# A decode kernel that streams its K and V cache: the MLP's weights first, sums in four column groups, and other sizes for wo and the last V

## The chip, the core and the metric

The kernel runs on one NeuronCore of a Trainium2 chip. The metric is the time of one execution in device microseconds: 1358.99 us, the median of three runs (1357.01 to 1359.01). A NeuronCore has a matrix engine (TensorE, PE in the profile, with PEld for its weight loads), VectorE (DVE), ScalarE (ACT), GpSimd (POOL) and SyncE (SP), which here does nothing but issue transfers. Sixteen DMA engines move data between HBM and the on-chip memory SBUF. Each engine works through its own instructions in order and waits for others by semaphores; an SP that waits for one transfer's buffer issues none of the transfers behind it. The matrix engine's sums go to PSUM.

## The reference

Two rows of activations x (2 x 1024, bf16) go through two branches, and a gate mixes them.

```python
def _A_ref(x, k_cache, v_cache, wq, wo):
    B, Sq, D = x.shape                       # 2, 1, 1024
    H, Dh = 32, 128
    q = (lambda x, *d: x.transpose(*d))((x @ wq).reshape(B, Sq, H, Dh), 0, 2, 1, 3)
    scores = jnp.einsum("bhqd,bhkd->bhqk", q, k_cache) * (Dh ** -0.5)
    p = _softmax(scores, axis=-1)            # over 16384 keys
    o = jnp.einsum("bhqk,bhkd->bhqd", p, v_cache)
    return (lambda x, *d: x.transpose(*d))(o, 0, 2, 1, 3).reshape(B, Sq, H * Dh) @ wo
...
    h = _gelu(_layernorm(x, axis=-1) @ w1)   # then h's four quarters are shifted along S
    hs = jnp.concatenate([g0, g1, g2, g3], axis=-1) @ w2
    x1 = x + hs
    h2 = _gelu(_layernorm(x1, axis=-1) @ w3) @ w4
    return x1 + h2
...
    g = _sigmoid((x * gate_w).sum(-1, keepdims=True))
    return g * a + (1 - g) * b
```

K and V are 2 x 32 x 16384 x 128 in bf16, 268 MB each. wq and wo are 1024 x 4096 and 4096 x 1024, w1 and w2 1024 x 1024, w3 and w4 1024 x 3584 and 3584 x 1024. The sequence has one position, so every shifted quarter of h is zero, and so is hs: the kernels multiply a zero row (shT) by w2 all the same.

## The kernel before

**Units.** The cache is worked through in 32 units: a pair of heads of one batch row, 16 pairs x 2 rows. A unit's K is 8.39 MB and lies in SBUF as 128 partitions of 64 KB; its V likewise. One large SBUF tile `mem` is cut into five cells of 32 KB per partition. K of even units takes cells 0 and 1, K of odd units cells 1 and 2, V cells 3 and 4.

**What a unit does.** `score_first` and `score_second` go through K in 8 chunks: VectorE turns a chunk in 32 x 32 blocks (L464, 2.28 us), TensorE multiplies it by q (L470, 8 matmuls of 512 columns). The half that lies in cell 1 goes first, since the next unit's K needs that cell. `softmax_a` finds the maxima; `pv` multiplies an earlier unit's probabilities by its V (64 matmuls, L542); `pv_end` scales the sums on ScalarE (osb) and brings them to a column per head by 4 matmuls with lane selectors (L560); `softmax_b` makes the exponentials. pv of unit n - 2 runs in unit n, after which the next V may be loaded. After each second unit `wo_project` (L432) adds the pair's two heads times wo into `arow`, two PSUM rows of 512 columns each.

**The MLP** lies inside units 0 and 1. w1 and w2 take cell 2, w3 takes the cells of wq after the q projection, w4 those of w3. A layer accumulates in `oacc`, four rows r at a time in four groups of 32 partitions (L210, `wide_bank`), is copied to `wide`, and is summed over the groups and turned by one fp32 matmul with a 128 x 128 left side for each 128 outputs (L241; L275 for q). `layernorm_T`, `gelu_T` and the gate are short chains of small instructions. The fourth layer and the residual reach `arow` by L409.

**The order of transfers** is the order in which SP meets them: wq, x, gate_w, K of unit 0, w1, w2; w3 after the q projection; K1, wo of four heads, w4, K2, V0, K3, V1 and so on: K and V alternate. wo comes four heads at a time, 2 KB to a row. From unit 29 six small reads of gate_w ("probe", L447) are issued among the others; all write the same tile, so each waits for the one before to land. The last V is cut in eleven pieces (32, 32, 32, 32, 32, 32, 16, 16, 16, 8, 8 of 256 columns j) that go to cells 3 and 4, and the last wo pair comes behind them. `pv_last` multiplies the first 96 columns as `pv` does and the other 160 with V as the left side (L587). Two copies (L643, L645) and two output transfers end the program.

Of the kernel before, what the change touches and what calls it, by code (L numbers as in the profile page):

```python
# [10 lines left out]
FP32 = mybir.dt.float32  # L11
# [12 lines left out]
def kernel(  # L24
# [26 lines left out]

# [4 lines left out]
    CT = 32  # L56
# [6 lines left out]
    assert NJ % CT == 0 and CT % GT == 0 and NG <= QP  # L63
# [3 lines left out]
    wopool = ctx.enter_context(tc.tile_pool(name="wopool", bufs=1))  # L67
# [3 lines left out]
    sps = ctx.enter_context(tc.tile_pool(name="sps", bufs=2, space=PSUM))  # L71
    ops = ctx.enter_context(tc.tile_pool(name="ops", bufs=1, space=PSUM))
    rps = ctx.enter_context(tc.tile_pool(name="rps", bufs=1, space=PSUM))
# [8 lines left out]
    def region(cell, elements):  # L82
        return mem[:, cell * CELL : cell * CELL + elements]

    k_cell = [0 if u % 2 == 0 else 1 for u in range(NU)]
    v_cell = [3] * NU
    v_cell[NU - 2] = 0
    units = [(hp, b) for hp in range(HP) for b in range(B)]

    def cache_rows(cache, u):  # L90
        hp, b = units[u]
        return cache[b, 2 * hp : 2 * hp + 2].rearrange("h s d -> (h s) d").rearrange(
            "(p j) d -> p (j d)", p=P
        )

    def load_k(u):
        nc.sync.dma_start(out=region(k_cell[u], NJ * Dh), in_=cache_rows(A_k_cache, u))

    def load_v(u):
        nc.sync.dma_start(out=region(v_cell[u], NJ * Dh), in_=cache_rows(A_v_cache, u))  # L100

    PIECES = [32] * 6 + [16] * 3 + [8] * 2
    assert sum(PIECES) == NJ

    def load_v_pieces(u):
        j = 0
        for n in PIECES:
            nc.sync.dma_start(
                out=region(v_cell[u], NJ * Dh)[:, j * Dh : (j + n) * Dh],
                in_=cache_rows(A_v_cache, u)[:, j * Dh : (j + n) * Dh],  # L110
            )
            j += n

    def k_view(u):
        return region(k_cell[u], NJ * Dh).rearrange("p (j d) -> p j d", d=Dh)

    def v_view(u):
        return region(v_cell[u], NJ * Dh).rearrange("p (j d) -> p j d", d=Dh)

    wq_t = region(3, KC * H * Dh).rearrange("p (r n) -> p r n", r=KC)  # L120
    nc.sync.dma_start(out=region(3, KC * H * Dh), in_=A_wq.rearrange("(p r) n -> p (r n)", p=P))
    xin = const.tile([P, B, KC], BF16)
    nc.sync.dma_start(out=xin[:], in_=A_x.rearrange("b s (p r) -> p (b s) r", p=P))
    gwT = const.tile([P, KC], BF16)
    nc.sync.dma_start(out=gwT[:], in_=gate_w.rearrange("(p r) -> p r", p=P))
    load_k(0)
# [12 lines left out]
    sel = const.tile([P, 4, Q4, QP], BF16)  # L139
    nc.gpsimd.memset(sel[:], 0.0)  # L140
    for v in range(4):
        w, e = divmod(v, 2)
        nc.gpsimd.affine_select(
            out=sel[:, v],
            in_=sel[:, v],
            compare_op=ALU.not_equal,
            fill=1.0,
            base=-(2 * QP * w + e),
            pattern=[[0, Q4], [-2, QP]],
            channel_multiplier=1,  # L150
        )
# [9 lines left out]
    )  # L161

# [11 lines left out]
    sel8 = const.tile([P, 8], FP32)  # L174
    nc.vector.tensor_reduce(
        out=sel8[:],
        in_=ident_f[:].rearrange("p (c k) -> p k c", k=QP)[:, 0:8, :],
        axis=AX.X,
        op=ALU.add,
    )  # L180
    oacc = [ops.tile([P, 4 * Dh], FP32, name=f"oacc{k}") for k in range(2)]
    for k in range(2):
        nc.vector.memset(oacc[k][:], 0.0)

    NW = 2
    WW = P + NG
    qw = []
    for k in range(NW):
        t = const.tile([P, 4, WW], BF16, name=f"qw{k}")
        nc.gpsimd.memset(t[:], 0.0)  # L190
        qw.append(t)
# [485 lines left out]
```

## Time and profile before

| | |
|---|---|
| runs, median (range) | 1358.99 us (1357.01 to 1359.01) |
| profiled execution, span | 1358.0 us |
| mean granted clock of TensorE | 0.785 |
| PE busy | 806.9 us, 59% |
| VectorE busy | 650.4 us, 48% |
| ScalarE busy | 133.5 us, 10% |
| GpSimd busy | 15.2 us, 1% |
| read from HBM | 572.53 MB, 422 GB/s over the span |
| queue q1 (SP's transfers), share of the 16 DMA engines | 98.1% |
| K transfers, issue to landing (median) | 28.2 us |
| V transfers, issue to landing (median) | 33.5 us |

The page cuts the span in 40 slices of 34 us and gives for each the busy tenths of an engine and the rate of the transfers. A window's row says the same for a chosen stretch: its length, the busy time of each engine with its number of instructions, the granted clock of TensorE (1.00 is full speed), the mean busy share of the DMA engines, and GB/s. A transfer is counted where its packets start, so a share of a short window can pass 1. In a timeline a row is the start, the duration, the engine, the line, the operation, and in brackets how long the engine had been idle and what ended that. A row of waits gives who waited for whom, the total, how often and the longest. Issue to landing holds the wait behind earlier transfers.

### The profile page before, as it was taken

The page shows a single profiled execution, that of the slowest core. Times are in us where ns is not written, and L with a number is a line of the kernel's source. Part 1 is how long each engine was busy: PE and PEld are TensorE (multiplying, and loading weights), DVE is VectorE, ACT ScalarE, POOL GpSimd, SP SyncE. Part 2 cuts the span into 40 slices and gives each one's busy share as a digit, 9 for nine tenths or more (in the row PEclk, how much of TensorE's full clock was granted, in tenths as well). Part 3 has the DMA queues.
Part 4 walks back from the last instruction along what each step waited for, and adds up shares of the span by engine and source line. Part 5 has one row for each costly group of instructions (what it writes and reads, how often), then busy time and mean ns, then how long its engine had stood idle before and what let it go on. Part 6 is the DMA issues. An engine that isn't in the chain of part 4 may idle for free.

```text
span 1358.0 us, 11505 instructions
## 1 busy us (share of the span) xinstructions
PE 806.9 (59%) x5086; PEld 366.8 (27%) x5086; DVE 650.4 (48%) x511; ACT 133.5 (10%) x208; POOL 15.2 (1%) x54
## 2 busy tenths in 40 slices
PE   2897855555665545566555556655456665555564
PEld 1463422222222222222222222222222222222222
DVE  1436654444555534455544445555344555444450
ACT  0011011111100111110011111001111100111110
POOL 1000000000000000000000000000000000000000
PEclk9977877778876768888777788877678886777886
DMA  9987999999999999999999999999999999999996
GB/s 402 433 360 315 431 433 433 431 431 427 433 433 432 424 438 433 435 435 426 436 433 433 431 429 433 431 431 428 433 431 429 433 427 432 435 435 435 425 424 277
DMA packets 16183, 573.26 MB, mean 422 GB/s; under 512 B 1922, under 2 KB 1926, under 8 KB 6662
## 3 DMA queue, kind: packets, MB, share of 16 engines
q1 hardware_dynamic: 16130, 572.54, 98.1%
q8 instruction: 39, 0.64, 0.2%
q14 instruction: 10, 0.08, 0.0%
q10 hardware_dynamic: 4, 0.00, 0.0%
HBM read 572.53 MB, written 0.00 MB: 422 GB/s over the span
## 4 chain that ended last, share of the span: by engine, by line
DMA 67%; PE 17%; DVE 12%; issue 3%; ACT 0%; SPq 0%; POOL 0%; DVEq 0%; ACTq 0%
DMA mem<-in_A_k_cache_dram 57%; PE S L470 12%; DVE KT L464 11%; DMA probe<-in_gate_w_dram 7%; PE misc L241 2%; DMA xin<-in_A_x_dram 2%; PE oacc L210 1%; PE misc L275 1%; DMA wo<-in_A_wo_dram 1%; DMA mem<-in_A_v_cache_dram 0%; PE oacc L542 0%; PE arow L409 0%; ACT pt L509 0%; ACT mem L201 0%; DVE wide L203 0%
## 5 line engine op out<-in xcount | busy, mean ns | idle before, releaser
L470 PE MATMUL S<-KT,qw 128*128 128x512 bf16 x2048 | 551.9, 420 | 385.0 <-DVE KT L464 384.6
L464 DVE STREAM_TRANSPOSE KT<-mem 128x2048 f32<-128x2048 f32 x256 | 571.4, 2283 | 297.3 <-DMA mem<-in_A_k_cache_dram 243.6
L470 PEld LDWEIGHTS <-qw 128*128 128x128 bf16 x2048 | 219.8, 108 | 711.0 <-issue 537.0
L542 PE MATMUL oacc<-mem,pt 128*8 128x512 bf16 x2008 | 115.5, 382 | 8.6 <-DMA mem<-in_A_v_cache_dram 8.6
L495 ACT ACTIVATE Dm<-ident_s,m 128x128 f32<-128x128 f32 x32 | 12.8, 401 | 983.6 <-DVE m L493 983.6
L509 ACT ACTIVATE pt<-St,nb 64x256 bf16<-64x256 f32 x64 | 89.7, 1402 | 73.3 <-DVE nb L507 65.7
L572 DVE TENSOR_SCALAR OT<-misc,g_rep 128x2 bf16<-128x2 f32 x31 | 6.9, 222 | 140.5 <-PE misc L560 140.5
L520 PE MATMUL misc<-rs,lmat 128*128 128x1 f32 x62 | 17.8, 356 | 87.0 <-ACT pt L509 87.0
L542 PEld LDWEIGHTS <-pt 128*8 128x8 bf16 x2008 | 46.2, 87 | 74.5 <-issue 23.6
L522 DVE RECIPROCAL rinv<-misc 128x1 f32<-128x1 f32 x31 | 5.2, 168 | 101.6 <-PE misc L520 101.6
L491 DVE STREAM_TRANSPOSE St<-S 128x512 f32<-128x512 f32 x32 | 22.9, 717 | 63.7 <-PE S L470 63.7
L560 PE MATMUL misc<-sel,osb 128*128 128x2 f32 x256 | 34.5, 257 | 26.7 <-ACT osb L555 26.7
L560 PEld LDWEIGHTS misc<-sel,osb 128*128 128x128 f32 x256 | 31.8, 195 | 42.9 <-ACT osb L555 42.9
L520 PEld LDWEIGHTS misc<-rs,lmat 128*128 128x128 f32 x62 | 15.1, 303 | 97.9 <-ACT pt L509 97.7
L509 ACT ACTIVATION_READ_ACCUMULATOR pt<-St,nb 64x1 f32 x64 | 30.6, 478 | 0.0
L555 ACT ACTIVATE osb<-oacc,rinv 128x512 f32<-128x512 f32 x31 | 21.3, 687 | 69.0 <-PE oacc L542 69.0
L210 PE MATMUL oacc<-mem,xT 128*2 128x512 bf16 x64 | 9.4, 612 | 24.0 <-DVE xT L266 23.2
L307 POOL TENSOR_TENSOR qw<-qd,mask 128x16 bf16<-128x16 bf16 x32 | 8.4, 266 | 1180.9 <-PE S L470 1137.3
L507 DVE TENSOR_REDUCE nb<-misc 64x1 f32<-64x64 f32 x64 | 14.2, 222 | 5.0 <-PE misc L501 0.9
L275 PEld LDWEIGHTS misc<-sel,wide 128*128 128x128 f32 x64 | 14.2, 328 | 7.4 <-issue 4.4
L203 DVE COPY wide<-oacc 128x512 f32<-128x512 f32 x7 | 4.8, 691 | 22.9 <-PE oacc L210 22.9
L501 PE MATMUL misc<-Dm,ones_f 128*128 128x128 f32 x64 | 15.6, 326 | 0.0
(96 smaller groups left out, 168.3 us busy)
## 6 DMA issues: line engine op xcount, KB each, us to landing
mem<-in_B_w_dram SPq DMA_DIRECT2D x2, 7168.0 KB, 25.0
wo<-in_A_wo_dram SPq DMA_DIRECT2D x7, 1024.0 KB, 32.8
mem<-in_A_v_cache_dram SPq DMA_DIRECT2D x6, 1024.0 KB, 5.9
mem<-in_B_w_dram SPq DMA_DIRECT2D x2, 2048.0 KB, 45.9
mem<-in_A_v_cache_dram SPq DMA_DIRECT2D x3, 512.0 KB, 14.3
wo<-in_A_wo_dram SPq DMA_DIRECT2D x2, 512.0 KB
mem<-in_A_k_cache_dram SPq DMA_DIRECT2D x32, 28.2
mem<-in_A_v_cache_dram SPq DMA_DIRECT2D x2, 256.0 KB, 14.0
```

The source lines that it names most:

```text
L210: nc.tensor.matmul(acc[QP * q : QP * q + B, :], lhsT=actT[:, r, :], rhs=weight[:, r, :], start=(r < Q4), stop=(r >= R - Q4),)
L241: nc.tensor.matmul(ps[:, c, :], lhsT=wide.rearrange("p (m c) -> p c m", c=self.C)[:, c, :], rhs=sel8[:, 0:B], start=True, stop=True,)
L275: nc.tensor.matmul(qps[:, j * HB + k, :], lhsT=qo[:, k * Dh : (k + 1) * Dh], rhs=sel8[:, 0:B], start=True, stop=True,)
L464: nc.vector.transpose(out=kt[:], in_=Kc.rearrange("p j d -> p (j d)").bitcast(FP32))
L470: nc.tensor.matmul(S, lhsT=t[:, v, NG - 1 - m : NG - 1 - m + P], rhs=ktb[:, half * GT : (half + 1) * GT, w, :, e], start=(first and n == 0 ...
L491: nc.vector.transpose(out=st[:].rearrange("p j r -> p (j r)"), in_=S[:])
L501: nc.tensor.matmul(R_ps[:], lhsT=ones_f[:], rhs=Dm[:], start=True, stop=True)
L509: nc.scalar.activation(out=Pt[rows, :, e, :].rearrange("p (m a) k -> p a k m", a=GT // 4), in_=st[rows, :, 0:NG].rearrange("p (a k) m -> p ...
L520: nc.tensor.matmul(tot_ps[:, 0:1], lhsT=lmat[:], rhs=rs[:], start=True, stop=True)
L542: nc.tensor.matmul(acc[QP * q : QP * q + 8, :], lhsT=pts[u % NP][:, g].rearrange("p h k -> p (h k)"), rhs=v_view(u)[:, 4 * g : 4 * g + 4, ...
L555: nc.scalar.activation(out=osb[:], in_=oacc[u % 2][:], func=ACTF.Copy, scale=rinvs[u % NP][:, 0:1] if scaled else 1.0,)
L560: nc.tensor.matmul(ot[:], lhsT=osb[:, k * Dh : (k + 1) * Dh], rhs=sel8[:, k : k + 5 : 4], start=(k == 0), stop=(last and k == 3),)
```

## The change

- **Start.** x and gate_w are issued by ScalarE's queue. SP issues w1, w2 (cell 0), w3 (cells 1 and 2) and wq (cells 3 and 4) first, all without a wait; then K of unit 0 (cells 0 and 1, when w1 to w3 have been used), w4 (when wq has been used), K of unit 1, V of unit 0, the first wo pair. The gate, both layer norms and the first three layers come before the q projection and before any score; the fourth layer (`mlp_last`) stands in unit 0 behind its scores, and the residual times 1 - g (x1g) is added to `arow` ahead of the third layer.
- **Sums in column groups.** `rows4` gives each of the four 32-partition groups a quarter of the output's columns, so that every group holds finished sums. They are turned by one VectorE transpose (`turned`) instead of 128 x 128 matmuls. `arow` becomes one PSUM tile of 256 columns in four groups, written by 8 matmuls of 256 columns for a pair (`project`) and by 112 for the fourth layer (28 rows x 4 groups).
- **Units.** pv of unit n - 1 runs in unit n. V of unit n is issued behind it. The halves of a unit are put into `odd_rest` and `even_unit`; K and V still alternate in the queue.
- **wo** comes a pair at a time as 128 rows of 4 KB (two neighbouring rows of wo in a partition) into one buffer, `wo_pair`, issued after the previous pair's `project`. So that the columns fit, `pv_end` splits even and odd lanes: 16 small fp32 matmuls with 64 columns of left side, for 4 with 128. Pair 15 is fetched this way too, but is used from a second transfer in the old layout (`wo_last`).
- **End.** The last V goes to cells 0 and 1 in five pieces of 128, 64, 32, 16 and 16 columns; 192 columns go as in `pv`, 64 with V as the left side. wo's last pair goes to cell 3. One copy and two output transfers of four rows of 512 bytes end the program. The probes are gone.

```diff
-    k_cell = [0 if u % 2 == 0 else 1 for u in range(NU)]
-    v_cell = [3] * NU
-    v_cell[NU - 2] = 0
-    units = [(hp, b) for hp in range(HP) for b in range(B)]
...
-    PIECES = [32] * 6 + [16] * 3 + [8] * 2
...
+    xin = const.tile([P, B, KC], BF16)
+    nc.scalar.dma_start(out=xin[:], in_=A_x.rearrange("b s (p r) -> p (b s) r", p=P))
+    gwT = const.tile([P, KC], BF16)
+    nc.scalar.dma_start(out=gwT[:], in_=gate_w.rearrange("(p r) -> p r", p=P))
+
+    def load_weight(W, cell, offset=0):
+        K, N = W.shape
+        dst = region(cell, K // P * N, offset)
+        nc.sync.dma_start(out=dst, in_=W.rearrange("(p r) n -> p (r n)", p=P))
+        return dst.rearrange("p (r n) -> p r n", n=N)
+
+    w1 = load_weight(B_w1, 0)
+    w2 = load_weight(B_w2, 0, KC * D)
+    w3 = load_weight(B_w3, 1)
+    wq = load_weight(A_wq, 3)
+
+    K_CELL = (0, 1)
+    V_CELL = 3
...
-    nc.sync.dma_start(out=region(3, KC * H * Dh), in_=A_wq.rearrange("(p r) n -> p (r n)", p=P))
-    xin = const.tile([P, B, KC], BF16)
-    nc.sync.dma_start(out=xin[:], in_=A_x.rearrange("b s (p r) -> p (b s) r", p=P))
-    gwT = const.tile([P, KC], BF16)
-    nc.sync.dma_start(out=gwT[:], in_=gate_w.rearrange("(p r) -> p r", p=P))
-    load_k(0)
...
+    def rows4(acc, actT, weight, R, at, n, G):
         for r in range(R):
...
+            for g in range(Q4):
                 nc.tensor.matmul(
+                    acc[QP * g : QP * g + B, 0:n],
+                    lhsT=actT[:, r, :],
+                    rhs=weight[:, r, g * G + at : g * G + at + n],
+                    start=(r == 0),
+                    stop=(r == R - 1),
                 )
...
+    def turned(wide, C):
+        t = mlp.tile([P, C, QP], FP32, tag="turn", name="turn")
+        nc.vector.transpose(
+            out=t[:].rearrange("p c k -> p (c k)"), in_=wide.rearrange("p c k -> p (c k)")
+        )
+        return t[:, :, 0:B]
+
+    def layer(actT, weight, k):
+        rows4(oacc[k], actT, weight, KC, 0, G1, G1)
+        wide = mlp.tile([P, KC, QP], FP32, tag="wide", name="wide")
+        nc.scalar.activation(
+            out=wide[:], in_=oacc[k][:, 0:G1].rearrange("p (i r) -> p r i", r=KC), func=ACTF.Copy
+        )
+        return turned(wide[:], KC)
...
+    compute_gate()
+    layernorm_T(xT[:], xn1T[:], "ln1")
+    h1 = gelu_T(layer(xn1T, w1, 0), KC)
+    nc.vector.tensor_copy(out=hT[:], in_=h1[:])
+
+    nc.vector.memset(shT[:], 0.0)
...
+    nc.vector.tensor_tensor(out=x1T[:], in0=layer(shT, w2, 1), in1=xT[:], op=ALU.add)
+    layernorm_T(x1T[:], xn2T[:], "ln2")
+
+    for k in range(2):
+        rows4(oacc[k], xn2T, w3, KC, k * (G3 // 2), G3 // 2, G3)
+    wide3 = mlp.tile([P, FC, QP], FP32, tag="wide", name="wide")
+    for k in range(2):
...
+    wo_pair = const.tile([P, 2, D], BF16, name="wo_pair")
+
+    def load_wo(hp):
+        rows = A_wo[bass.ds(hp * 2 * Dh, 2 * Dh)]
+        nc.sync.dma_start(
+            out=wo_pair[:].rearrange("p t n -> p (t n)"),
+            in_=rows.rearrange("(p t) n -> p (t n)", p=P),
+        )
...
+    def project(oT, weight, last):
+        for t in range(2):
+            for g in range(Q4):
                 nc.tensor.matmul(
+                    arow[QP * g : QP * g + B, :],
+                    lhsT=oT[:, t, :],
+                    rhs=weight[:, t, g * G1 : (g + 1) * G1],
+                    start=False,
+                    stop=(last and t == 1),
+                    skip_group_check=True,
+                )
...
+    def mlp_last(w4):
+        for r in range(KC):
+            for g in range(Q4):
+                nc.tensor.matmul(
+                    arow[QP * g : QP * g + B, :].rearrange("b (i r) -> b r i", r=KC)[:, r, :],
+                    lhsT=x1g[:, r, :],
+                    rhs=ident_f[:, QP * g : QP * (g + 1)],
+                    start=(r == 0),
                     stop=False,
                     skip_group_check=True,
                 )
+        for r in range(FC):
+            for g in range(Q4):
                 nc.tensor.matmul(
+                    arow[QP * g : QP * g + B, :],
+                    lhsT=h2T[:, r, :],
+                    rhs=w4[:, r, g * G1 : (g + 1) * G1],
                     start=False,
+                    stop=False,
                     skip_group_check=True,
                 )
...
+    def pv_end(b):
+        osb = pv_rows(b, True)[:].rearrange("p (k d t) -> p k t d", k=4, t=2)
+        ot = misc_psum([P, 2])
+        for t in range(2):
+            for k in range(4):
+                for h in range(2):
+                    nc.tensor.matmul(
+                        ot[h * HALF : (h + 1) * HALF, t : t + 1],
+                        lhsT=osb[:, k, t, :],
+                        rhs=lane[:, k + 4 * h : k + 4 * h + 1],
+                        start=(k == 0 and t == 0),
+                        stop=(k == 3),
+                        skip_group_check=True,
+                    )
+        nc.vector.tensor_scalar(
+            out=oT[:, :, b], in0=ot[:], scalar1=g_rep[:, b : b + 1], scalar2=None, op0=ALU.mult
+        )
...
+    PIECES = (128, 64, 32, 16, 16)
+    MOVED = sum(PIECES[:2])
...
-    for n in range(NU):
-        score_first(n)
-        if n == 0:
-            compute_gate()
-            layernorm_T(xT[:], xn1T[:], "ln1")
-            lin1.compute(wide4())
-            mlp_post1()
-            lin2.compute(wide4())
-            mlp_post2()
-        if n + 1 < NU:
-            load_k(n + 1)
-        else:
-            load_v(NU - 2)
-        score_second(n)
-        softmax_a(n)
-        if n == 0:
-            lin3.compute(region(0, 2 * F).bitcast(FP32))
-            gelu_T(lin3.acc[:], h2T[:], FC)
-            load_wo(0, WOH)
-            lin4.load()
-        elif n == 1:
-            lin4.compute(wide4())
-            mlp_post4()
-            load_v(0)
-        else:
-            pv(n - 2)
-            if n < NU - 1:
-                load_v(n - 1)
-            else:
-                load_v_pieces(NU - 1)
-            pv_end(n - 2)
-            if n == NU - 3:
-                load_probes()
-            if n == NU - 1:
-                load_wo(H - 2, 2)
-        softmax_b(n)
-        if n % 4 == 1 and n > 1:
-            load_wo(n - 1, min(WOH, H - 2 - (n - 1)))
-    pv(NU - 2)
-    pv_end(NU - 2)
-    pv_last(NU - 1)
...
+    load_k(0, 0)
+    w4 = load_weight(B_w4, 3)
+
+
+    score_first(0, 0)
+    load_k(0, 1)
+    score_second(0)
+    softmax_a(0)
+    mlp_last(w4)
+    load_v(0, 0)
+    softmax_b(0)
+
+    def odd_rest(hp):
+        load_k(hp + 1, 0)
+        score_second(1)
+        softmax_a(1)
+        pv(0)
+        load_v(hp, 1)
+        pv_end(0)
+        softmax_b(1)
+
+    def even_unit(hp):
+        score_first(hp, 0)
+        load_k(hp, 1)
+        score_second(0)
+        softmax_a(0)
+        pv(1)
+        load_v(hp, 0)
+        pv_end(1)
+        project(oT, wo_pair, False)
+        load_wo(hp)
+        softmax_b(0)
+        score_first(hp, 1)
+
+    load_wo(0)
+    score_first(0, 1)
+
+    def last_unit(hp):
+        V_LAST = 0
+        load_v(hp, 1, V_LAST, PIECES)
+        score_second(1)
+        wo_last = region(V_CELL, 2 * D).rearrange("p (h n) -> p h n", h=2)
+        softmax_a(1)
+        pv(0)
+        pv_end_apart(0)
+        nc.sync.dma_start(
+            out=wo_last, in_=A_wo[(H - 2) * Dh : H * Dh].rearrange("(h d) n -> d h n", d=Dh)
+        )
+        softmax_b(1, by_head=True)
+        pv_last(1, V_LAST)
+        project(OTl, wo_last, True)
+        nc.vector.tensor_copy(out=out_row[:], in_=arow[:])
+        rows = out.rearrange("b s (g n) -> (b s) g n", g=Q4)
+        for b, queue in enumerate((nc.sync, nc.scalar)):
+            queue.dma_start(
+                out=rows[b], in_=out_row[:].rearrange("(g k) n -> k g n", k=QP)[b]
+            )
+
...
+        for i in range(HP - 1):
+            odd_rest(i)
+            even_unit(i + 1)
+        last_unit(HP - 1)
```

## The prediction

> **What bounds the kernel now.** I read the page's strip of the span first, then stretches by window, then the DMA issues of SP (SyncE) in order of time, then the waits. The strip says that the DMA engines are the bound nearly everywhere, at about 433 GB/s, and that it falls short at the start (slice 1), in slices 3 and 4, and in the last.
>
> ```profile
> DMA  9987999999999999999999999999999999999996
> GB/s 402 433 360 315 431 433 433 431 431 427 433 433 432 424 438 433 435 435 426 436 433 433 431 429 433 431 431 428 433 431 429 433 427 432 435 435 435 425 424 277
> ```
>
> The windows (busy time of each engine, then granted clock, DMA share, GB/s) put sizes on them:
>
> ```profile
> 50.00:90.00 40.00, 33.71 (x163) 17.05 (x166) 24.24 (x35) 2.30 (x5) 1.69 (x4) 0.87 0.90 380
> 110.00:160.00 50.00, 39.98 (x215) 20.09 (x216) 34.71 (x27) 4.04 (x9) 0.27 (x1) 0.82 0.82 349
> 160.00:1310.00 1150.00, 668.51 (x4131) 285.00 (x4130) 578.10 (x408) 112.99 (x174) 7.47 (x28) 0.78 1.00 432
> 1310.00:1345.00 35.00, 19.82 (x258) 10.87 (x256) 3.28 (x10) 5.18 (x8) 0.00 (x0) 0.73 0.86 360
> 1325.00:1334.00 9.00, 4.22 (x52) 1.56 (x55) 0.00 (x0) 0.00 (x0) 0.00 (x0) 0.57 0.57 229
> 1345.00:1358.00 13.00, 4.53 (x100) 3.19 (x100) 0.84 (x2) 0.59 (x1) 0.00 (x0) 0.50 0.54 208
> ```
>
> From 160 to 1310 us the engines of DMA never rest: 432 GB/s, share 1.00. Against 432 the three gaps are worth 40 x (1 - 380/432) = **4.8 us** (gap A), 50 x (1 - 349/432) = **9.6 us** (gap B) and 35 x (1 - 360/432) = **5.8 us** (gap C). The last 13 us lose 6.7 us to the closing sum and the output. What SP issues, and when, explains A and B:
>
> ```profile
> 71.72 0.33 SPq L97 DMA_DIRECT2D mem<-in_A_k_cache_dram  x1
> ...
> 92.71 0.33 SPq L232 DMA_DIRECT2D mem<-in_B_w_dram  x1
> 121.69 0.33 SPq L97 DMA_DIRECT2D mem<-in_A_k_cache_dram  x1
> ```
>
> Gap A is the second K transfer, which needs the cells of w1 and w2 and comes at 71.72. Gap B is the third: it comes at 121.69, 29 us after w4's issue, because the third MLP layer's sums hold TensorE and VectorE:
>
> ```profile
> 93.36 12.86 PE L241 MATMUL misc<-sel,mem 128*128 128x2 f32 x56 [0.70 <-ACT mem L201]
> ```
>
> Gap C is SP again. A probe transfer waits for the landing of the one before, which stands behind 8 MB in the queue; the pieces of the last V wait behind the probe:
>
> ```profile
> SPq L447 <- DMA probe<-in_gate_w_dram: 36.3, 5, 14.6
> ```
> ```profile
> 1313.16 0.33 SPq L108 DMA_DIRECT2D mem<-in_A_v_cache_dram  x1
> 1328.15 0.31 SPq L447 DMA_DIRECT2D probe<-in_gate_w_dram  x1
> 1328.52 0.33 SPq L108 DMA_DIRECT2D mem<-in_A_v_cache_dram  x1
> 1332.41 0.33 SPq L447 DMA_DIRECT2D probe<-in_gate_w_dram  x1
> 1332.78 6.07 SPq L108 DMA_DIRECT2D mem<-in_A_v_cache_dram  x9
> ```
>
> Compute has room in the steady part: VectorE waits 226.1 / 27 = 8.4 us for K in every unit:
>
> ```profile
> DVE KT L464 <- DMA mem<-in_A_k_cache_dram: 226.1, 27, 10.7
> ```
>
> **The change, part by part.** The bytes are all but the same, so the question is whether SP always issues the next transfer before the queue runs dry. How early must that be? x was issued behind wq and was used at 22.94; wq was issued at 0.79 and is 8.39 MB, 19.4 us at 432 GB/s. So issue to landing is 22.94 - 0.79 - 19.4 = 2.7 us beside the data. I ask for 2.7 us of lead, which is on the safe side.
>
> *Start.* w1, w2, w3, wq go out without a wait. Landings: 0.8 + 2.7 + 4.9 = 8.4, 13.2, 30.2 (7.34 MB, 17.0 us) and 49.6 us. Then, one after the other:
> - K0 takes the cells of w1, w2, w3, so it waits for the third layer's last matmul and is due by 49.6 - 2.7 = 46.9. Before w3 lands: the two layer norms took 4.2 us (48.65 to 52.79) and 3.4 us (83.97 to 87.40); layers 1 and 2 are 32 matmuls each, at most 147 ns (the q projection's row, L210 on xT: 9.4 us for 64), 4.7 us; the residual's 32 fp32 matmuls into arow now stand here, 3.1 us by L409. If x lands in the first microseconds this ends near 25 us, under w3. The third layer: 64 x 147 ns = 9.4 us, so K0 is issued at 39.6, 7 us early.
> - w4 waits for q's 64 matmuls: 49.6 + 9.4 = 59.0, due 66.3. The q that the scores need follows within about 3 us (two copies of 0.6, two transposes of 0.7, small casts), before K0 lands at 69.0.
> - K1 waits for the first half of K0's scores. In the steady part that is 11.2 us (K landed 1249.59, next K issued 1260.74): 80.2, due 83.3.
> - V0 waits for the fourth layer: scores end 21.8 us after landing (1249.59 to 1271.4), at 90.8, then 112 matmuls of 256 columns. At 57 ns (the row of the same layer before, L210 on h2T: 3.2 us for 56) 6.4 us: 97.2, due 102.7. At 147 ns it is 107.3, 4.6 us late. I take 57: TensorE comes straight from 64 score matmuls, as it did in that row, while the 147 came after rest.
> - K2: K1 lands at 105.4, plus 11.2 is 116.6, due 122.
>
> So gaps A and B go: **-14.4 us**, bounds -14.4 and -5 (V0 late by 4.6 and K0 by as much). Where layers now turn by a VectorE transpose instead of 128x128 fp32 sums, 56 + 48 + 64 fp32 matmuls of 0.23 us go from TensorE; nothing waits for them any more, beyond gap B.
>
> *Steady part.* K, V and half-unit order are as before (V one unit sooner, but queued at the same place). pv_end has 16 fp32 matmuls for 4. The row L560 has 8 records a unit, so two passes each: 24 passes more, 24 x 131 ns (1.05 us for 8) = 3.1 us, or 24 x 257 ns (its mean duration, unpipelined) = 6.2 us. Both lie under the 8.4 us of waiting; it would cost time from 350 ns a pass on. Queued behind pv_end: the sum of maxima and the exponentials (softmax_b), whose result is needed a unit later. load_wo waits on SP for the project matmuls; these end about 25.5 (V's issue after K's landing) + 0.7 + 4.2 + 0.6 = 31 us after a landing, while the next K can't be issued before 38.7 + 11.2: 19 us of room. **0**. wo moves 4 KB rows for 2 KB, and pair 15 is fetched twice: +0.52 MB, 1.2 us. The longer rows can gain at most what the stretch loses against 433, the strip's commonest figure: 1150 x (1 - 432/433) = 2.7 us. **0**, bounds +1.2 and -1.5, between which nothing in the trace chooses.
>
> *End.* The probes go, and the last V goes to the K cells 0 and 1, cell 0 long free, cell 1 11.2 us after K31's landing, while V30 and wo's pair 15 keep the queue for 19.4 + 1.2 us. Gap C gives back at least 9 x (1 - 0.57) = 3.9 us (the hole itself) and at most 5.8; five pieces remain small for eleven, so I take **-5.0**. The last V piece still lands ahead of wo's 0.5 MB, and the sum waits for wo as before; the output copy has 256 columns for 512, 0.68 us to about 0.35: **-0.3**.
>
> *Sum.* The profiled execution: 1358.0 - 14.4 - 5.0 - 0.3 = 1338.3 us of span. The median of the runs, 1358.99, is 1.0 above that span: **1339.3**.
>
> **Rivals.**
> 1. *A part of the gap comes back in the start*: V0 4.6 us late (matmuls at 147 ns), or K0 about 5 us late because x and the gate row come through between the weights' long rows and the gate's sum stands first on TensorE. For it: PE's clock was 0.50 to 0.87 in the windows around there. Against: 3 to 7 us of room at each step. 1339.3 + 4.7 = 1344.
> 2. *x starves* (slower). x and gate_w now come by ACT's queue beside four weight transfers. If they land only behind all four, at 49.6, then norm 4.2, two layers 9.4, copy and transpose 1.3, norm 3.4 + 3.1, third layer 9.4 stand before K0: 80.4 for 46.9, 33.5 us late, 1373. Break-even is 19.7 us late, x at about 36 us. For it: x's 22.9 us in the trace before, on SP's queue. Against: the instruction queue q8 got 39 packets through beside a queue that holds 98.1% of the engines, and no engine shows a wait for instructions. The Trainium skill (DMA: Bandwidth & Descriptors, Queues, rings and completion order) has each DMA engine go round the queues packet by packet, by which x comes after at most a part of w1 and w2; no run here shows that yet for ACT's queue.
> 3. *A fixed price per transfer* (slower): wo's 17 transfers for 9 in the steady part, each exposed at 2.7 us: 8 x 2.7 = 21.6, 1361; it decides from 2.5 us each. Against: the stretch 160 to 1310 carries over 60 transfers, seven of wo's, at 432 GB/s; issued early, none shows a hole. The Trainium skill (DMA: Bandwidth & Descriptors, Anatomy of one DMA and Rules for kernel authors) asks for 1 MiB or more per DMA and states about 2.0 us fixed beside the data; as an estimate by that page 16 us, 1355, if exposed. The trace puts that time under other transfers.
>
> **How the numbers follow.** The forecast 0.74, its own range 1336 to 1342 (gap C's bounds, wo's, a microsecond of new edges). Rival 1: 0.14. Rival 2: 0.05. Rival 3: 0.03. Something unseen 0.04: half of it faster, a quarter each the same and slower. The range 1335.5 to 1349 holds the first two. 0.2% is 2.7 us, about what a measurement can tell. Faster: 0.74 + 0.14 + 0.02 = 0.90; slower 0.05 + 0.03 + 0.01 = 0.09; same 0.01.
>
> **What would show it.** Right: no window of 10 us from 2 us to the last V piece under about 400 GB/s; K0 issued near 40 us, w4 near 59, K1 near 80, V0 near 97; SP waits for DVE and PE, never for a probe; DVE's wait for K still 2 to 6 us a unit. Wrong: xT written late (past 25 us); a hole before K0 or V0; a hole in every unit before K, with TensorE in the lane sums; or a steady rate below 430 GB/s with no hole.

## The result, and the profile after

The changed kernel takes **1342.89 us** (median of four runs, 1342.64 to 1343.09) where the kernel before takes 1359.0 us in the same runs (1357.01 to 1359.68): a ratio of 0.9886, 95% interval 0.9872 to 0.99, or 16 us less. A second group of runs on another chip gave 1342.96 us (1342.38 to 1344.12), ratio 0.9897 (0.988 to 0.9913). The forecast was 1339.3, so the sign, the mechanism and most of the size came true, and 3.6 us did not. The span fell from 1358.0 to 1340.8 us, by 17.2.

The strip of the changed kernel (DMA share in tenths and GB/s, 40 slices):

```profile
DMA  9999999999999999999999999999999999999997
GB/s 407 433 419 438 436 435 423 437 423 438 431 433 436 427 435 431 428 436 435 427 440 435 429 432 423 436 433 437 425 435 433 426 434 421 438 431 440 421 427 316
```

The low slices 1, 3 and 4 of before are gone; the transfers rest only in the last slice. The windows say the same in numbers (busy time of PE, PEld, DVE, ACT and POOL with instruction counts, granted clock, DMA share, GB/s):

```profile
50.00:90.00 40.00, 18.92 (x124) 7.60 (x125) 21.46 (x23) 1.44 (x3) 0.43 (x2) 0.79 0.98 422
110.00:160.00 50.00, 31.88 (x197) 13.38 (x196) 28.73 (x19) 3.90 (x6) 0.27 (x1) 0.78 1.03 442
160.00:1310.00 1150.00, 667.20 (x4883) 288.65 (x4883) 575.73 (x407) 112.99 (x174) 7.44 (x28) 0.78 1.00 431
1310.00:1328.00 18.00, 12.82 (x118) 5.88 (x120) 7.47 (x11) 3.90 (x6) 0.00 (x0) 0.87 0.98 417
1328.00:1337.00 9.00, 6.54 (x116) 3.83 (x112) 0.16 (x1) 0.60 (x1) 0.00 (x0) 0.69 0.52 210
```

Gap A's window is at 422 GB/s (380 before), gap B's at 442 (349). Gap C's place is at 417, and what follows, 1328 to 1337, is no hole but a slope: by the completion records of the last transfer seven of the DMA engines are done between 1329.7 and 1330.5 us and the other nine between 1333.3 and 1336.8.

SP's issues in order of time (start, duration, line, tile) show how the start is kept full:

```profile
47.98 0.33 SPq L108 DMA_DIRECT2D mem<-in_A_k_cache_dram  x1
54.94 0.33 SPq L92 DMA_DIRECT2D mem<-in_B_w_dram  x1
81.61 0.33 SPq L108 DMA_DIRECT2D mem<-in_A_k_cache_dram  x1
95.50 0.33 SPq L115 DMA_DIRECT2D mem<-in_A_v_cache_dram  x1
...
118.44 0.33 SPq L108 DMA_DIRECT2D mem<-in_A_k_cache_dram  x1
```

The forecast had 39.6, 59.0, 80.2, 97.2 and 116.6. Only the first is far off: K of unit 0 goes out 8.4 us late. VectorE's first two instructions on x and gate_w (start, duration, tile; in brackets the idle time before and what ended it) show why:

```profile
13.87 0.17 DVE L218 COPY xT<-xin 128x16 bf16<-128x16 bf16 x1 [9.88 <-DMA xin<-in_A_x_dram]
...
30.90 0.17 DVE L224 TENSOR_TENSOR xg<-xin,gwT 128x16 f32<-128x16 bf16 x1 [16.65 <-DMA gwT<-in_gate_w_dram]
```

x was there at 13.9 us, when w2 had landed, and the 2 KB of gate_w at 30.9, when w3 had. The gate's sum is the first work on TensorE (its matmul starts at 31.33), so both layer norms and three layers waited for it.

In the steady part VectorE still waits for K (total, times, longest; the window from 160 to 1310 us): 241.5 / 29 = 8.3 us a unit, as before.

```profile
DVE KT L420 <- DMA mem<-in_A_k_cache_dram: 241.5, 29, 10.5
```

### The profile page after: what moved, and what is told of

It reads as the page before. It is cut to its first block, busy times and chain, and to the rows that moved or that the text cites. A ratio compares the mean times of both kernels' runs of the same rounds, so it can differ in the third digit from the quotient of the medians.

```text
span 1340.8 us, 12847 instructions
## 1 busy us (share of the span) xinstructions
PE 755.4 (56%) x5758; PEld 329.9 (25%) x5758; DVE 648.7 (48%) x511; ACT 129.6 (10%) x202; POOL 12.8 (1%) x47
## 4 chain that ended last, share of the span: by engine, by line
DMA 72%; DVE 12%; PE 12%; issue 4%; POOL 0%; ACT 0%; ACTq 0%; DVEq 0%
DMA mem<-in_A_k_cache_dram 68%; DVE KT L420 11%; PE S L426 11%; DMA gwT<-in_gate_w_dram 2%; DMA mem<-in_A_wo_dram 1%; PE oacc L194 0%; POOL ln_rstd L265 0%; PE misc L259 0%; DVE spread L165 0%; PE misc L245 0%; DVE turn L204 0%; PE arow L378 0%; PE misc L230 0%; ACTq L85 0%; DVE out_row L620 0%
## 5 line engine op out<-in xcount | busy, mean ns | idle before, releaser
L426 PE MATMUL S<-KT,qw 128*128 128x512 bf16 x2048 | 546.3, 416 | 414.4 <-DVE KT L420 414.1
L475 PE MATMUL misc<-rs,lmat 128*128 128x1 f32 x62 | 18.2, 362 | 93.4 <-ACT pt L464 93.4
L525 DVE TENSOR_SCALAR oT<-misc,g_rep 128x2 bf16<-128x2 f32 x30 | 6.7, 222 | 129.1 <-PE misc L517 129.1
L517 PE MATMUL misc<-lane,osb 128*64 128x1 f32 x960 | 33.8, 199 | 25.5 <-ACT osb L505 25.5
L517 PEld LDWEIGHTS misc<-lane,osb 128*64 128x64 f32 x960 | 31.3, 138 | 40.7 <-ACT osb L505 40.7
L357 POOL TENSOR_TENSOR qw<-qdu,mask 128x16 bf16<-128x16 bf16 x32 | 8.4, 265 | 1184.7 <-PE S L426 1170.5
L449 DVE TENSOR_REDUCE m<-St 128x1 f32<-128x256 f32 x32 | 13.4, 420 | 1.1
L457 PEld LDWEIGHTS misc<-Dm,ones_f 128*128 128x128 f32 x64 | 9.6, 189 | 0.7 <-issue 0.2
```

Source lines behind the costliest of these rows:

```text
L426: nc.tensor.matmul(S, lhsT=qw[b][:, v, NG - 1 - m : NG - 1 - m + P], rhs=ktb[:, half * GT : (half + 1) * GT, w, :, e], start=(first and n ...
L449: nc.vector.tensor_reduce(out=m[:], in_=st[:, :, 0:NG], axis=AX.XY, op=ALU.max)
L457: nc.tensor.matmul(R_ps[:], lhsT=ones_f[:], rhs=Dm[:], start=True, stop=True)
L475: nc.tensor.matmul(tot_ps[:, 0:1], lhsT=lmat[:], rhs=rs[:], start=True, stop=True)
L517: nc.tensor.matmul(ot[h * HALF : (h + 1) * HALF, t : t + 1], lhsT=osb[:, k, t, :], rhs=lane[:, k + 4 * h : k + 4 * h + 1], start=(k == 0 a ...
```

## The experiments

The kernels of one group share a chip and the runs of the kernel before. There are three groups: the two kernels of gap C with x first and wo once; the two holes with x late and the second kernel of the end; and the others, with the unaltered changed kernel (1342.96 us). "Before" and "changed" in a heading say which kernel was edited.

### Gap C by itself (before, edited)

The first kernel drops the probes; the second also cuts the last V in five pieces, as the change does.

```diff
-            if n == NU - 3:
-                load_probes()
```
```diff
-    PIECES = [32] * 6 + [16] * 3 + [8] * 2
+    PIECES = [128, 64, 32, 16, 16]
...
-        moving = sum(PIECES[:3]) // 4
+        moving = sum(PIECES[:2]) // 4
```

> The kernel before without its six probe transfers, nothing else. Forecast's reading of gap C (mean share of the DMA engines: the hole from 1325 to 1334 us is worth 3.9 us): 1359.0 - 3.9 = 1355.1 us. Rival reading (the sixteen DMA engines run up to 6 us apart by then, a transfer lands with its slowest engine, and the hole is mostly the waiting of the fast ones): from the landing of the last K at 1290.9 to the end of the DMA the kernel before needs 62.0 us where three V transfers, the pieces' overhead and wo need about 61.1, so about -0.9 us: 1358.1 us.

> The kernel before without the probes and with the last V in five pieces (128, 64, 32, 16, 16 columns, 192 of them as moving rows) instead of eleven. Forecast's step for gap C as a whole: 1359.0 - 5.0 = 1354.0 us. Rival reading: -0.9 for the hole and about -1 for eight-kilobyte rows and smaller that become longer: 1357.1 us.

Measured: 1356.88 us (1355.07 to 1357.76), ratio 0.9995 (0.9986 to 1.0004), and 1356.03 (1354.15 to 1357.55), ratio 0.9987 (0.9978 to 0.9996), beside 1357.77 for the kernel before: 0.9 and 1.7 us less. The interval of the first (1.9 us less to 0.5 more) includes no change at all; that of the second is 0.5 to 3.0 us less. Yet the hole itself went. The windows of the kernel without probes:

```profile
1310.00:1345.00 35.00, 19.74 (x273) 10.52 (x272) 3.24 (x10) 5.18 (x8) 0.00 (x0) 0.73 0.97 409
...
1325.00:1334.00 9.00, 4.39 (x56) 1.60 (x59) 0.00 (x0) 0.00 (x0) 0.00 (x0) 0.57 0.98 411
```

The share from 1325 to 1334 rose from 0.57 to 0.98, and the whole window from 360 to 409 GB/s. Priced as the prediction did, that is 35 x 49 / 432 = 4.0 us. One execution of each, from the last K's use to the last wo matmuls, gives 2.75 us (1290.91 to 1353.90 is 62.99; without probes 1290.79 to 1351.03 is 60.24) and 3.3 us with five pieces; the runs give less. So the gap existed and was closed, but with the pieces it was worth 0.5 to 3.0 us by the runs, not 3.9 to 5.8. Single executions of the kernel before scatter over 4.7 us, so these runs give the size no closer. The trace of before shows where the share misleads: from 1326 to 1330 us eight or nine of the sixteen engines still had packets in flight, and only from 1333 to 1335 us were nearly all at rest.

### What a hole is worth (changed, edited)

If a mean DMA share overstates a hole, a hole made on purpose should show by how much, and whether it matters when it comes. Swapping the two halves of one unit's scores holds back the next K. It was done in unit 4 and in unit 28.

```diff
-        score_chunks(b, halves[1 - b], True, False)
+        now[b] = 2 * hp + b
+        score_chunks(b, halves[b if now[b] in FLIP else 1 - b], True, False)
...
-        score_chunks(b, halves[b], False, True)
+        score_chunks(b, halves[1 - b if now[b] in FLIP else b], False, True)
```

with `FLIP = (4,)` and `(28,)`.

> The changed kernel, with the two halves of unit 4's scores in the other order, so that the next K may be asked for only when all of unit 4's K is read: 19.7 us after its landing (one transfer takes 19.4, starting one 1.0 us more) instead of 11.0. The queue of the slowest DMA engine runs dry for about 1.5 us; that of the others for as much as they are ahead, up to 1.8 us at this place, so the mean share loses about 2.4 us. Reading by the mean share: 1342.9 + 2.4 = 1345.3 us. Reading by the slowest engine: 1342.9 + 1.5 = 1344.4 us. If the time hangs on something else than the queue: 1342.9.

> The same edit at unit 28, where the engines' landings of one transfer lie up to 7 us apart. The mean share loses 1.5 + about 3.5 = 5 us. Reading by the mean share: 1342.9 + 5 = 1347.9 us, 2.6 us over the early one. Reading by the slowest engine: the same 1.5 us as the early one, 1344.4 us or less, and a last landing with less spread.

Measured: 1346.8 us (1345.99 to 1347.19) and 1346.03 (1344.83 to 1346.54), ratios 0.9918 (0.9903 to 0.9933) and 0.9913 (0.9896 to 0.9929): 3.8 and 3.1 us above the changed kernel's 1342.96, or 2.9 and 2.2 us by the ratios, since the two ran on another chip. The expectations had 1345.3 or 1344.4 for the early one and 1347.9 or 1344.4 for the late one, so neither reading came out. The windows of the early hole, and then of the late one:

```profile
278.00:284.00 6.00, 4.82 (x23) 2.12 (x22) 6.00 (x5) 0.40 (x1) 0.26 (x1) 1.00 0.79 335
284.00:286.00 2.00, 1.60 (x8) 0.58 (x6) 1.94 (x4) 1.12 (x2) 0.00 (x0) 1.00 0.37 150
286.00:288.00 2.00, 0.45 (x4) 0.20 (x3) 1.44 (x1) 1.72 (x4) 0.00 (x0) 1.00 0.01 2
288.00:295.00 7.00, 6.04 (x28) 2.46 (x27) 6.49 (x4) 0.00 (x0) 0.00 (x0) 1.00 1.13 449
```
```profile
1222.00:1229.00 7.00, 5.76 (x26) 2.32 (x24) 7.00 (x5) 0.00 (x0) 0.26 (x1) 1.00 0.89 384
1229.00:1235.00 6.00, 4.44 (x20) 1.79 (x18) 5.94 (x6) 2.02 (x4) 0.00 (x0) 1.00 0.44 184
1235.00:1237.00 2.00, 0.72 (x5) 0.48 (x6) 1.09 (x2) 1.22 (x2) 0.00 (x0) 1.00 0.71 236
1237.00:1245.00 8.00, 7.05 (x35) 2.72 (x34) 7.84 (x4) 0.00 (x0) 0.00 (x0) 1.00 1.04 434
```

By shares the early hole loses 6 x 0.21 + 2 x 0.63 + 2 x 0.99 - 7 x 0.13 = 3.6 us and costs 3.8; the late one loses 7 x 0.11 + 6 x 0.56 + 2 x 0.29 - 8 x 0.04 = 4.4 us and costs 3.1. The early one falls steeply and empties at once. The late one has a long half-full stretch first, in which some engines rest and others still have work. A transfer is there when its slowest engine is done, so the rest of the fast engines costs nothing; the share counts it as lost. Both holes cost 1.5 to 1.7 us more than the time in which the trace shows all engines at rest (about 2.1 and 1.6 us), so that reading is too low by itself. What the pair supports is the direction: late in the run a mean share overstates a hole, 4.4 us for 3.1 here, while early it fits, 3.6 for 3.8. The runs of the two kernels overlap (1345.99 to 1347.19 and 1344.83 to 1346.54), so it is not settled by them alone; gap C points the same way.

### The start (changed, edited)

First x and gate_w were put ahead of the weights on SP's queue, then behind the four weights.

```diff
-    nc.scalar.dma_start(out=xin[:], in_=A_x.rearrange("b s (p r) -> p (b s) r", p=P))
+    nc.sync.dma_start(out=xin[:], in_=A_x.rearrange("b s (p r) -> p (b s) r", p=P))
...
-    nc.scalar.dma_start(out=gwT[:], in_=gate_w.rearrange("(p r) -> p r", p=P))
+    nc.sync.dma_start(out=gwT[:], in_=gate_w.rearrange("(p r) -> p r", p=P))
```

In the second kernel these lines stand behind the load of wq.

> The changed kernel with x and gate_w first on SP's queue instead of on ScalarE's beside the weights. Both readings: x and the gate row are used near 4 us instead of 13.9 and 30.9, the first K is issued near 35 us instead of 48.0, and the time stays at 1342.9 (1342.4 to 1343.9: w1 is issued 0.9 us later), if the first K left no hole. If it came too late by a hidden microsecond or two: 1341 to 1342.

> The changed kernel with x and gate_w on SP's queue behind all four weights, the starvation of rival 2. They land near 50 us; from the landing of the gate row to the first K's issue the changed kernel took 48.0 - 30.9 = 17.1 us, so the first K is issued near 67 us for about 49, when the queue runs dry: a hole of 18 us, all engines alike. 1342.9 + 18 = 1361 us, slower than the kernel before. The prediction's own chain would give 1373. If the first K does not bound the start: 1342.9.

Measured: 1343.03 us (1342.98 to 1343.09), ratio 0.9892 (0.9879 to 0.9906), with K0 issued at 37.38; and 1361.46 us (1360.94 to 1361.63), ratio 1.0025 (1.0014 to 1.0035). SP's issue of K0, VectorE's copy of x and a window of the second:

```profile
67.26 0.33 SPq L108 DMA_DIRECT2D mem<-in_A_k_cache_dram  x1
```
```profile
50.09 0.18 DVE L218 COPY xT<-xin 128x16 bf16<-128x16 bf16 x1 [44.69 <-DMA xin<-in_A_x_dram]
```
```profile
50.00:68.00 18.00, 10.78 (x178) 6.26 (x182) 5.14 (x29) 1.84 (x6) 1.40 (x2) 1.00 0.02 9
```

In the first, K0 issued 10.6 us earlier gives the same time, so the 8.4 us by which K0 was late cost little. That they cost nothing is not shown: with x and gate_w ahead of it w1 goes out 1.00 us later (1.79 for 0.79), and yet K0 is first used at 71.28, beside 71.10 in the changed kernel, so up to 0.8 us may lie hidden. The second shows what the gain hangs on. x is used at 50.09, K0 goes out 17.2 us later, the queue is dry for 18 us, and all of the gain is lost, 18.5 us. Rival 2's place and sign were right, its price (1373) was too high, since the chain from x to K0 took 17.2 us and not 30.8.

### The end (changed, edited)

The last wo pair is fetched once, ahead of the last V, so that nothing lands behind V (first kernel). The second also cuts the last V in 128, 64, 32, 16, 8 and 8 columns, with only 128 going as in `pv`. The third adds x and gate_w first on SP's queue.

```diff
-        load_wo(hp)
+        if hp < HP - 1:
+            load_wo(hp)
+        else:
+            nc.sync.dma_start(
+                out=wo_pair[:], in_=A_wo[(H - 2) * Dh : H * Dh].rearrange("(h d) n -> d h n", d=Dh)
+            )
...
-        project(OTl, wo_last, True)
+        project(OTl, wo_pair, True)
```
```diff
-    PIECES = (128, 64, 32, 16, 16)
-    MOVED = sum(PIECES[:2])
+    PIECES = (128, 64, 32, 16, 8, 8)
+    MOVED = PIECES[0]
```

> The changed kernel, with wo's last pair fetched once, in the layout of the end, into the one wo buffer behind the previous pair, so that no transfer follows the last V. By its bytes (0.52 MB at 432 GB/s) 1.2 us off 1342.9: 1341.7 us. If the last landing is set by the slowest DMA engine the same 1.2 us, since each engine carries a sixteenth. If the sum at the end waits for other work than that transfer: 1342.9.

> The kernel with wo's last pair fetched once, and the last V in pieces of 128, 64, 32, 16, 8, 8 columns of which only the first 128 go as moving rows. In the kernel with wo fetched once alone, TensorE waited 1.2 us for the second piece, and then 16 matmuls, a copy, 8 slow fp32 matmuls (1.87 us) and 64 more (1.84 us) stood in a row up to the end. Here the copy and the fp32 sums lie behind the first piece and are done before the second lands, so the end should follow the last landing: 1.2 us for wo and about 0.5 us of the end off 1342.9, 1341.2 us. If that row of matmuls was not what held it: 1343.6, as with wo fetched once alone.

> The changed kernel with three small edits together: x and gate_w ahead of the weights on SP's queue, wo's last pair fetched once and before the last V, and the last V in pieces of 128, 64, 32, 16, 8 and 8 columns with 128 moving. If the end is set by when the last piece lands and what follows it, the pieces give back their 0.3 us and the start nothing: 1342.3 to 1342.6 us. If the hole of some 0.8 us that single executions show near 49 us was worth its mean, 1341.5 to 1342.0.

> The changed kernel itself, unaltered, to have its time beside the other kernels of this group on one chip. Expected 1342.9 us (1342.6 to 1343.3), as the changed kernel's own runs gave (1342.64 to 1343.09).

Measured: 1343.65 us (1342.93 to 1343.94), 1342.55 (1342.36 to 1342.81) and 1342.33 (1342.21 to 1342.69), with ratios 0.9896 (0.9883 to 0.991), 0.9888 (0.9873 to 0.9903) and 0.9891 (0.9876 to 0.9906); the unaltered changed kernel 1342.96, on the chip of the third. Half a megabyte less at the very end, 1.2 us of transfer, gained nothing. TensorE's rows of the first kernel show what takes its place:

```profile
1331.67 1.88 PE L492 MATMUL oacc<-mem,pt 128*8 128x512 bf16 x16 [1.20 <-DMA mem<-in_A_v_cache_dram]
...
1334.31 1.87 PE L539 MATMUL misc<-lane,osb 128*128 128x2 f32 x8 [0.76 <-ACT osb L505]
...
1336.04 1.84 PE L548 MATMUL misc<-pt,mem 128*128 128x2 bf16 x64
```

From the second piece's landing on, TensorE works in series, 1.88 + 1.87 + 1.84 us with the copy to osb between, and no transfer is waited for any more. A good part of that is the clock: the granted clock is 0.50 here from 1331 to 1336 us, while in the changed kernel it is 1.00 from 1331 to 1333 us, and the same 16 and 8 matmuls take 1.04 and 1.05 us there. So this kernel does not show what the half megabyte is worth by itself. Nor was 1.2 us to be had: in the changed kernel the closing sum waits 0.70 us for wo, and where no wo comes last it still waits 0.25 us for the copy of OTl, which leaves 0.45.

With fewer columns in that chain (second and third kernel, clock 1.00 and 0.99 from 1331 to 1333 us) the end follows the transfers again. The medians are 0.4 and 0.6 us lower, where the expectation for the second had 1.7, and the ranges of the runs touch (1342.36 to 1342.81, 1342.21 to 1342.69, unaltered 1342.38 to 1344.12), so even this gain is not sure.

### The price of a transfer (changed, edited)

Every V but the last in two transfers of half the columns, 31 transfers more.

```diff
-    def load_v(hp, b, cell=V_CELL, pieces=(NJ,)):
+    def load_v(hp, b, cell=V_CELL, pieces=(NJ // 2, NJ // 2)):
```

> The changed kernel with every V but the last fetched in two transfers of 128 columns each instead of one (the same bytes, 31 transfers more). By the prediction's rival of a fixed price of 2.7 us for each transfer: 31 x 2.7 = 84 us more, 1427 us; by the Trainium skill's fixed 2 us, as an estimate (DMA: Bandwidth & Descriptors, Anatomy of one DMA), 62 us more, 1405 us. By the reading that queued transfers hide what each costs: 1342.9 us, at most 1 us above.

Measured: 1345.28 us (1345.02 to 1345.64), ratio 0.9912 (0.9898 to 0.9927), 2.3 us more than the unaltered kernel on the same chip. That is 75 ns for each of 31 transfers, and no window shows a hole (431 GB/s from 160 to 1310). It was not nothing, but a thirty-sixth of rival 3's 2.7 us. The fixed 2.0 us of the Trainium skill (DMA: Bandwidth & Descriptors, Anatomy of one DMA), which that section fits to transfers that GpSimd issues, do not appear for these of SP: whatever each costs lies under other transfers here. Whether the 75 ns go with the transfers or with their shorter rows (32 KB for 64 KB) was not told apart.

### More work on TensorE (changed, edited)

The sixteen lane matmuls of `pv_end` are done five times over; the sums stay the same.

```diff
-        for t in range(2):
-            for k in range(4):
...
+        for again in range(5):
+            for t in range(2):
+                for k in range(4):
...
```

> The changed kernel with the sixteen lane matmuls at the end of every unit done five times over, which leaves the same sums. The profile gives 1.13 us for one set, so TensorE gets 4 x 1.13 = 4.5 us more in each of 32 units. If the steady part is bound by the transfers, that lies under the 8.3 us of each unit in which VectorE waits for K, and only the last unit shows it: 1342.9 + 4.5 = 1347.4 us at most if the last unit's stand in series. If the units were bound by computing, 31 x 4.5 = 140 us more, 1483 us. If the price per matmul were that of the kernel before (131 ns each), 8.4 us per unit, the cover would just be used up, and the time would grow by some us.

Measured: 1349.57 us (1349.35 to 1349.7), ratio 0.9944 (0.9929 to 0.9959), 6.6 us more. The waits and the window of the steady part, and the instruction queue (packets, MB, share of the engines):

```profile
DVE KT L420 <- DMA mem<-in_A_k_cache_dram: 70.3, 28, 4.5
```
```profile
160.00:1310.00 1150.00, 836.39 (x8578) 452.91 (x8576) 571.21 (x405) 112.96 (x174) 7.50 (x28) 0.77 1.00 430
```
```profile
q8 instruction: 75, 1.23, 0.4%
```

TensorE's busy time grew by (836.39 - 667.20) / 29 = 5.8 us a unit, and the wait for K shrank by as much, from 8.3 to 2.5. So the cover was real and not used up: computing did not become the bound, which would have cost well over 100 us. And yet 6.6 us came on top, more than the 4.5 that the expectation allowed, while the end of the program has no lane matmul of this kind to show. It is the transfers that ended later, by 7 us. In the changed kernel the instruction queue moved 45 packets (0.74 MB), and in the kernel before 39. The 1920 matmuls that the edit adds (64 in each of 30 units; 3840 records, two passes each) brought 30 packets of 16 KB more, and each of these holds one of the sixteen DMA engines for 1.05 us (the mean of their records in the trace). What that does to the time is taken up in the last section.

## Why the prediction was right, and where it was wrong

**Where the 17.2 us are.** VectorE's first use of the last K, and the closing wo matmuls, of the kernel before:

```profile
1290.91 2.31 DVE L464 STREAM_TRANSPOSE KT<-mem 128x2048 f32<-128x2048 f32 x1 [9.70 <-DMA mem<-in_A_k_cache_dram]
```
```profile
1353.90 1.01 PE L432 MATMUL arow<-wo,OT 128*2 128x512 bf16 x4 [0.92 <-DMA wo<-in_A_wo_dram]
```

and of the changed kernel:

```profile
1295.38 2.31 DVE L420 STREAM_TRANSPOSE KT<-mem 128x2048 f32<-128x2048 f32 x1 [8.00 <-DMA mem<-in_A_k_cache_dram]
```
```profile
1336.87 0.60 PE L378 MATMUL arow<-mem,OTl 128*2 128x256 bf16 x8 [0.70 <-DMA mem<-in_A_wo_dram]
```

By its last K the changed kernel has moved one V more, 19.4 us of transfer, and is only 4.47 us later: 14.9 us saved up to there. The K of unit 3 parts the start from the steady part (before, then changed):

```profile
183.62 4.51 DVE L464 STREAM_TRANSPOSE KT<-mem 128x2048 f32<-128x2048 f32 x2 [7.78 <-DMA mem<-in_A_k_cache_dram]
```
```profile
186.20 4.51 DVE L420 STREAM_TRANSPOSE KT<-mem 128x2048 f32<-128x2048 f32 x2 [7.88 <-DMA mem<-in_A_k_cache_dram]
```

There it is one V less half a megabyte of wo ahead, 7.86 MB or 18.2 us, and 2.58 us later: 15.6 us were saved by then, and 0.7 us was lost again up to the last K. (A second profile of the changed kernel, with this K at 186.73 and the last at 1295.54, gives 15.1 and 0.3.) From the last K to the wo matmuls it takes 41.49 us against 62.99 - 19.4 = 43.6: 2.1 us. From there to the end 3.9 against 4.1: 0.2 us. Together 17.2.

| step of the prediction | forecast | measured |
|---|---|---|
| gaps A and B, up to K of unit 3 | -14.4 | -15.6 |
| steady part, from there to the last K | 0 | +0.7 (wait for K 8.3 us a unit, as before) |
| gap C, with pair 15 fetched twice | -5.0 | -2.1 in the profiles; the probes and pieces alone -0.9 and -1.7 in the runs |
| end | -0.3 | -0.2 |
| span to median of the runs | +1.0 | +2.1 |

**Gaps A and B: right**, and for the reason given: SP no longer waits until the queue is dry. That more than the two gaps came back has a place in the trace of before: from 20 to 50 us it moved 404 GB/s, 1.9 us by the same sum, which stood in no term. The start's schedule held within 4 us but for K0. There the chain from x was forecast too slow and the arrival of gate_w too early, and the two all but cancelled: K0 was issued at 47.98 against a due time of 46.9. That the closest step of all held was luck. The layers took less than their bounds (the third 4.6 us for 64 matmuls, forecast 9.4; the fourth's 112 matmuls 3.2 us, forecast 6.4 at 57 ns each from a row of 512 columns, where the new ones have 256), and V0 went out at 95.50 rather than late. Of rival 1 the second half happened, rows of gate_w between those of w3, but it cost at most about 0.8 us (x and gate_w first: 1343.03).

**The steady part: right in the sum but for 0.7 us, too dear in the working.** The sixteen small matmuls of pv_end were priced at 3.1 to 6.2 us more per unit, and VectorE's wait for K was to shrink to 2 to 6 us; it stayed at 8.3. They cost nothing: the row of L517 has 33.8 us for 960 records, that of the four large matmuls before 34.5 for 256. A shape of 64 columns of left side and one of right side can't be priced by one of 128 and two. The cover would have held the price anyway, as the fivefold run shows.

**Gap C: the term that was mis-sized**, and with it the forecast. "Gap C gives back at least 9 x (1 - 0.57) = 3.9 us" took a mean share as time. Removing the same hole in the kernel before gave 0.9 us without the probes and 1.7 us with the pieces; the profiles 2.75 and 3.3. The engines were not all at rest in it. Besides, pair 15 is fetched twice in the stretch behind the last K, 1.2 us that stood in the prediction as the bound of another part and was taken as nothing. The two make up the change's figure: 3.3 us in the profile with five pieces, less 1.2, is the 2.1 of the table.

**Span to median.** The forecast added the 1.0 us by which the median of the runs exceeded the profiled span of before. Each run of the changed kernel exceeds its own span by 1.7 to 1.8 us (1342.64 for 1340.8), as does the kernel without probes (1356.88 for 1355.2). So the profiled execution of before was some 0.8 us slower than its median, that of the changed kernel 0.25 us faster, and the forecast took the one for typical.

Gap C's 2.9 us, the steady part's 0.7, the 0.1 at the end and the 1.1 here, less the 1.2 that A and B gave beyond the forecast, make the 3.6 us.

**The rivals.** x starving is the mechanism that decides the sign: made real, it gave 1361.46, slower than before. It did not happen, since ACT's queue has its turn beside SP's. How the turns go can be read from x and gate_w: their 16-byte rows came through one for each long row of the weights, x done with w2 at 13.87 us, gate_w done with w3 at 30.90. By the Trainium skill (DMA: Bandwidth & Descriptors, Queues, rings and completion order) each DMA engine goes round the queues it has work for; the trace agrees. That page has an engine drain typically some 9 to 17 descriptors in one turn, by which x, 16 rows to an engine, would have been through within the first turns; the trace shows one row in a turn. A fixed price of 2 us or more per transfer is ruled out by the split V, at 75 ns.

## What to carry to other kernels

Where the transfers are the bound, find each stretch in which the queue runs dry and ask what the queue's engine waited for just before; holes early in the run, when all DMA engines stop together, could be taken at their full length here (3.6 us by share for 3.8, and 18 us for 18.5 with x late). Late in the run take a low mean share as an upper bound, and look at whether all engines rest or only the fast ones. Two transfers that share the engines from different queues take turns row by row, so a tiny transfer of many small rows can be held as long as the large one beside it; sent first, it is not, though here that started the large transfer 1.0 us later.

## What was not expected of the hardware

**The sixteen DMA engines drift apart, and the drift goes with instruction fetches.** The completion records of one transfer's sixteen parts lie within 0.8 us at the start of the changed kernel and within 7.3 us for the last K, seven engines within 0.8 us and nine from 3.7 to 7.3 us behind. The spread does not grow evenly. It hardly moves between fetches, and the slowest engine falls back by 1.1 to 1.4 us at the fetches 1, 9, 17, 25, 33 and 41 of 45 (at 47, 257, 509, 749, 994 and 1234 us), as if eight engines took the fetches in turn; the other fetches move engines that are less far behind. After 12, 19 and 27 fetches the spread is 3.5, 4.9 and 6.4 us in the changed kernel (at 365, 583 and 820 us) and 3.3, 4.8 and 6.4 us in the kernel with lane matmuls fivefold (at 268, 388 and 526 us): the same spread at the same number of fetches, not at the same time. From about 6 us on it grows no further for long (5.3 to 8.1 us over the last 40 fetches of the fivefold kernel); that the fast engines then run out of queued work would fit, but was not traced. Why the fetches should fall on eight engines and not on all sixteen stays open, and so does what holds the ninth back. A hole brings the engines together again: behind the late one the parts of a K or V land within 1.5 to 1.6 us.

It also gives instructions a price that no engine's row shows. While it grows, the spread gains about 1.5 us with every eight fetches (1.8 us after 8, 3.3 after 16, 4.9 after 24, 6.4 after 32 in the changed kernel). As an estimate from that, the 30 further fetches are worth some 5.6 of the 6.6 us of the fivefold run. Its first K also went out 1.12 us later (49.10 for 47.98), for a reason that was not traced; together they are about what the run shows. By the same sum the change itself, with 45 fetches for 39, pays some 1.1 us over the whole program for its smaller matmuls; its steady part lost 0.3 to 0.7.
